# Twenty-four more zero products on TensorE around the first transposes and scores

## The chip, the cores and the metric

The kernel runs on one core of a Trainium2 chip. The metric is the device time of one execution in microseconds (us); lower is better. A core has five engines that run their own queues of instructions in order and wait for one another by semaphores: TensorE (PE in the profile, with its weight loads on a row of their own, PEld), VectorE (DVE), ScalarE (ACT), GpSimd (POOL) and SyncE (SP), which issues most of the transfers. TensorE's clock can be granted in full or in part; the profile shows the granted share.

## The reference

Two layers follow each other: cosine attention, then a feed-forward layer with a hard-swish. The shapes are 8 batches, 12 heads, 448 positions, 64 values per head; the feed-forward layer takes 3584 tokens of 768 values through 2048.

```python
q_n = q / (norm(q) + 1e-06)              # per position, over 64 values
k_n = k / (norm(k) + 1e-06)
attn = softmax(q_n @ k_n.T / tau)        # tau = 0.1
x = (attn @ v) -> [3584, 768]            # heads side by side
h = x @ w_in                             # [3584, 2048]
g = h * clip(h + 3, 0, 6) / 6
out = g @ w_out                          # [3584, 768]
```

## The kernel before

**Tiles.** The attention works on twins: twin `i` is two heads of a batch, six twins per batch, 48 in all. Two consecutive twins share one item of `q` and one of `k`; item `j` is one load of 128 x 896 values. For each item the kernel loads it (`LQ`), squares it (`SQ`, on ACT, DVE or POOL), sums the squares (`RE`, DVE, L310), makes 1 / norm of them (`NO`, four small ACT instructions, L326 to L329) and multiplies by it (`NM`, L341, into `nrm`). For the first items TensorE then transposes `nrm` (`TR`, seven products with the identity, L398, into the PSUM bank Y or Z), and DVE or ACT copies the result out to `tT` for q (`CQ`) and to `kz` for k (`CK`, L418 and L420).

For each twin the scores come in four groups: `SC.i.0` to `SC.i.3` (L502, and L499 for the last group) put the products of `kz` and `tT` into one of two pairs of PSUM banks named SC, the last number being the pair. `EX` (L521, ACT) takes the exponentials into `att`, `VA` (L537) multiplies them by the values `vx` into the accumulator PV, and `FI` (L557 and L558, DVE) divides by the sums. `VC` casts a twin's values into `vx` (L363 on POOL, L361 on DVE). `BK` and `CX` transpose the finished twin back into `xT`, from which the feed-forward layer's products (L671, L837, L1026) read. Weights are loaded by POOL (`W`, L1131).

**Order.** Nothing schedules the work: the list of strings `PLAN` is run word by word (L1198), and each word puts its instructions at the end of their engines' queues. A word such as `TR.1.Y` is an operation, a number and options; `a`, `v` or `p` names the engine (ACT, DVE, POOL). So an instruction's place in its engine's queue is its word's place in `PLAN`. Semaphores are set from the data that instructions share.

**The zero products.** The word `DP.n` calls `busy_pv(n)`. It issues `n` products of a block of zeros, 128 x 128 by 128 x 248, into columns of PV that nobody reads. The zeros lie in the first slice of `xT[1]`, which is not yet in use, and a memset at L1185 makes them.

```python
def busy_pv(n):
    first = ("VA", 0, 0) not in issued
    for _ in range(n):
        nc.tensor.matmul(
            PV[:, 0, 260:508], zeros[:, 0:128], zeros[:, 0:248], start=first, stop=first, skip_group_check=True
        )
```

Before the change there are 42 of them, all in the first 37 us: `DP.23` ahead of the first transpose `TR.0.Z`, `DP.10` ahead of `TR.1.Y`, `DP.3` after `SC.0.1`, `DP.2` ahead of `VA.0.0`, `DP.1` after `SC.1.3`, and `DP.3` ahead of `VA.5.0`.

Of the kernel before, what the change touches and what calls it, by code (L numbers as in the profile page):

```python
# [20 lines left out]
    "SQ.2.a.0.7 LQ.3 NM.0.v.0 NM.0.v.1 NO.0.1 DP.23 TR.0.Z RE.2 LQ.4 LQ.5 NM.1.p.0 NM.1.p.1 SQ.3.a.0.7 RE.3 SQ.5.p.0.7 DP.10 TR.1.Y CQ.0.a CK.0.v",  # L21
    "SQ.4.a.0.7 NO.1 CQ.1.a SC.0.0.0 NM.2.p EX.0.0 SC.0.1.1 EX.0.1 RE.4 DP.3 SC.0.2.0 W.0 LV.0 VC.0.p RE.5 CK.1.v SC.0.3.1 EX.0.2 NM.3.v LV.1 EX.0.3 NO.2",
    "VC.2.v W.2 TR.2.Z LQ.7 SC.1.0.0 EX.1.0 SC.1.1.1 EX.1.1 SQ.7.v.0.7 CQ.2.v VC.1.p DP.2 VA.0.0 VA.0.1 VA.0.2 SC.1.2.0 EX.1.2 VC.3.p NM.4.p VA.0.3 FI.0",
    "LQ.8 LQ.6 TR.3.Y CK.2.v SC.1.3.1 DP.1 SC.2.0.0 SQ.6.a.0.7 VA.1.0 VA.1.2 EX.1.3 SC.2.1.1 NM.5.p RE.7 EX.2.0 EX.2.1 CK.3.v VA.1.3 RE.6 SQ.8.p.0.7 VA.1.1",
    "SC.2.2.0 FI.1 EX.2.2 SC.2.3.1 EX.2.3 TR.4.Y VA.2.0 NO.3 LV.2 CQ.3.v SC.3.0.0 CQ.4.v CQ.5.v VC.4.v VA.2.1 VA.2.2 VA.2.3 SC.3.1.1 FI.2 TR.5.Z EX.3.0",
    "EX.3.1 CK.4.v BK.0.Y LV.3 LQ.9 RE.8 SC.3.2.0 SC.3.3.1 VA.3.0 EX.3.2 SC.4.0.0 EX.3.3 EX.4.0 CK.5.v CX.0.v SQ.9.v.0.7 VA.3.2 SC.4.1.1 VA.3.1 SC.4.2.0",
    "VA.3.3 FI.3 BK.2.Z CX.2.v EX.4.1 EX.4.2 NM.6.p TR.6.Y SC.4.3.1 EX.4.3 SC.5.0.0 EX.5.0 VA.4.0 RE.9 W.3 W.1 VA.4.3 SC.5.1.1 VC.6.p VA.4.2 VA.4.1 CQ.7.v",
    "CQ.6.v SC.5.2.0 EX.5.1 EX.5.2 NM.7.p TR.7.Z CK.6.v VC.5.p LQ.10 BK.3.Y CX.3.v SQ.10.p.0.7 SC.5.3.1 CS.7.v EX.5.3 NO.4 BK.1.Y FI.4 DP.3 VA.5.0 CS.6.v",
    "OPEN VA.5.2 SC.6.0 CX.1.v CK.7.v NM.8.p EX.6.0 VA.5.3 VA.5.1 FI.5 SC.6.1 EX.6.1 BK.4 CX.4.v SC.6.2 SC.6.3 EX.6.2 EX.6.3 BK.5 CX.5.v VA.6.0 VA.6.1 TR.8",
    "CQ.8.v CQ.9.v LQ.11 SQ.11.p.0.7 SC.7.0 VA.6.2 EX.7.0 VA.6.3 SC.7.1 SC.7.2 F.0.2 EX.7.1 EX.7.2 RE.11 RE.10 SC.7.3 EX.7.3 FA.0.2 F.0.7 FA.0.7 FI.6",  # L30
    "NM.9.p TR.9 CK.9.v CK.8.v CS.8.v CS.9.v F.0.1 LQ.14 LQ.13 SQ.13.a.0.7 NO.5 F.0.3 FA.0.1 FV.0.7 FV.0.2 FV.0.1 VC.7.p W.5 FA.0.3 LQ.12 LV.4 SQ.12.p.0.7",
    "SC.8.0 SC.8.1 FV.0.3 RE.12 LV.5 W.4 VC.8.p VA.7.0 EX.8.0 EX.8.1 NM.10.p F.0.0 FA.0.0 SC.8.2 VA.7.3 FV.0.0 VA.7.1 VA.7.2 VC.11.p EX.8.2 SC.8.3 EX.8.3",
    "SC.9.0 EX.9.0 F.0.4 RE.13 FI.7 SC.9.1 NM.11.p VC.10.p FA.0.4 FV.0.4 SC.9.2 TR.10 VA.8.0 VA.8.1 EX.9.1 NO.6 NM.13.p SC.9.3 CQ.11.v TR.11 CQ.10.v",
    "CS.11.v EX.9.2 EX.9.3 CK.11.v LQ.15 VA.8.2 F.0.6 VA.8.3 CS.10.v CK.10.v SC.10.0 FA.0.6 FV.0.6 EX.10.0 F.0.5 FA.0.5 SC.10.1 SC.10.2 SC.10.3 FI.8 VC.9.p",
    "VA.9.0 VA.9.2 VA.9.1 EX.10.1 EX.10.2 EX.10.3 FV.0.5 VA.9.3 FI.9 SC.11.0 EX.11.0 F.0.10 FA.0.10 FV.0.10 SQ.14.a.0.7 NM.12.p W.9 VA.10.0 TR.12 CQ.13.v",
    "CQ.12.v VA.10.1 SC.11.1 VA.10.3 SC.11.2 XP.6 VA.10.2 FI.10 EX.11.1 EX.11.2 F.0.14 FA.0.14 BK.8 SC.11.3 EX.11.3 CX.8.a BK.9 VA.11.0 TR.13 VA.11.2 RE.14",
    "CS.12.a CX.9.v LV.6 FV.0.14 CK.12.v CS.13.a CK.13.v F.0.15 FA.0.15 VC.12.p SQ.15.p.0.7 FV.0.15 SC.12.0 SC.12.1 RE.15 EX.12.0 EX.12.1 VA.11.1 F.0.13",
    "SC.12.2 VA.11.3 FI.11 FA.0.13 FV.0.13 BK.10 CX.10.a NO.7 F.0.12 FA.0.12 EX.12.2 F.0.9 W.8 LQ.16 SQ.16.v.6.1 SQ.16.p.0.6 RE.16 VA.12.0 BK.11 CX.11.v",
    "NM.15.p NM.14.p FV.0.12 F.0.8 LQ.20 LQ.17 LQ.19 SQ.17.a.0.7 RE.17 FA.0.8 SC.12.3 FV.0.8 G.6.0.p FA.0.9 FV.0.9 F.1.4 FA.1.4 EX.12.3 FV.1.4 F.1.1 FA.1.1",
    "FV.1.1 SC.13.0 SC.13.1 SQ.19.v.0.7 RE.19 EX.13.0 EX.13.1 LQ.18 SQ.18.p.0.7 F.1.5 FA.1.5 FV.1.5 LV.7 XD.15 XD.14 W.7 W.6 F.1.9 FA.1.9 FV.1.9 F.0.11",  # L40
    "VA.12.3 VC.13.a WS.7.1 FA.0.11 FV.0.11 F.1.15 FA.1.15 F.1.6 G.1.0.p G.2.0.p FA.1.6 RE.18 FV.1.15 CS.14.v FV.1.6 NO.8 NM.16.p F.1.8 SC.13.2 CK.15.v",
    "VA.12.1 LQ.21 SQ.21.p.0.7 VC.15.p SC.13.3 VA.12.2 FA.1.8 FV.1.8 FI.12 VC.14.a F.1.0 NM.17.v WS.y4.1 EX.13.2 EX.13.3 NO.9 F.1.10 CK.14.v FA.1.10",
    "FV.1.10 FA.1.0 NM.18.p GL.0.p FV.1.0 F.1.11 FA.1.11 SC.14.0 FV.1.11 EX.14.0 F.1.12 FA.1.12 FV.1.12 SC.14.1 SC.14.2 F.1.3 SQ.20.a.0.7 FA.1.3 G.7.0.v",
    "EX.14.1 EX.14.2 VA.13.0 VA.13.3 VA.13.2 VA.13.1 FI.13 FV.1.3 F.1.7 FA.1.7 FV.1.7 XD.16 SC.14.3 SC.15.0 VA.14.0 VA.14.2 VA.14.1 EX.14.3 EX.15.0 XD.17",
    "WS.6 SC.15.1 SC.15.2 VA.14.3 SC.15.3 EX.15.1 EX.15.2 F.1.2 FA.1.2 CK.16.v SC.16.0 EX.15.3 FI.14 CK.17.v FV.1.2 WS.y3 EX.16.0 LV.8 VC.16.a F.1.13",
    "FA.1.13 XP.12 LV.9 VA.15.0 VA.15.2 VA.15.3 SC.16.1 EX.16.1 SC.16.2 VA.15.1 NM.19.p CS.16.v XD.18 XD.19 FV.1.13 FI.15 F.1.14 FA.1.14 VC.17.a SC.16.3",
    "P.3.1 FV.1.14 LQ.22 XP.14 EX.16.2 WS.7.0 WS.y4.0 LQ.23 VA.16.0 SC.17.0 VA.16.1 G.5.0.p P.3.0 LV.11 RE.21 EX.16.3 VA.16.3 G.7.1.v EX.17.0 PE.3.1.a",
    "SC.17.1 SC.17.2 VA.16.2 CK.18.v PE.3.0.a EX.17.1 FI.16 XB.16 EX.17.2 P.5.0 PE.5.0.a SC.17.3 VA.17.0 RE.20 WS.1 VA.17.1 EX.17.3 SC.18.0 SC.18.1 EX.18.0",
    "EX.18.1 SC.18.2 VA.17.3 VA.17.2 G.5.1.p P.4.0 P.5.1.a FI.17 XB.17 NO.10 NM.20.v PE.4.0.v CK.19.v CS.18.v XD.20 LQ.24 LQ.25 VC.18.a P.1.0 P.7.0 EX.18.2",
    "BO.0 LV.10 SQ.22.a.0.7 G.1.1.p P.2.0 PE.2.0.a PE.1.0.v PE.7.0.v RS.0 SC.18.3 VA.18.0 NM.21.p XD.21 P.6.0 RE.22 PE.6.0.v SQ.23.a.0.7 RE.23 G.6.1.v",  # L50
    "LQ.26 VA.18.1 SC.19.0 EX.18.3 PE.5.1.a EX.19.0 VA.18.2 F.2.2 FA.2.2 FV.2.2 SQ.24.v.0.7 SC.19.1 SC.19.2 EX.19.1 EX.19.2 VA.18.3 FI.18 CK.21.v CK.20.v",
    "F.2.3 F.2.12 NO.11 FA.2.12 G.2.1.p FA.2.3 FV.2.3 NM.22.p LQ.27 PL.5.1 SC.19.3 FV.2.12 CS.20.v P.4.1 EX.19.3 XD.22 VC.19.v LV.12 F.2.13 FA.2.13 FV.2.13",
    "P.2.1.a F.2.14 VA.19.0 VA.19.2 F.2.5 NM.23.p LQ.28 XD.23 PE.2.1.a PE.4.1.v PL.2.1 VC.21.p BO.1 RS.1 SQ.25.a.0.7 F.2.11 VC.20.p RE.24 RE.25 VA.19.1",
    "FA.2.14 FV.2.14 FA.2.5 SQ.26.a.0.7 FA.2.11 F.2.6 FV.2.5 FV.2.11 VA.19.3 SC.20.0 SC.20.1 FA.2.6 FV.2.6 P.1.1 PE.1.1.v FI.19 EX.20.0 EX.20.1 SC.20.2",
    "VC.22.a NO.12 SC.20.3 F.2.9 CK.22.v FA.2.9 FV.2.9 EX.20.2 EX.20.3 P.6.1 PE.6.1.v F.2.7 XP.18 FA.2.7 FV.2.7 VA.20.0 VA.20.3 RE.26 SC.21.0 SC.21.1",
    "NM.24.v P.7.1 EX.21.0 LQ.29 LV.13 SC.21.2 SC.21.3 G.7.2.p NM.25.p VC.23.p EX.21.1 EX.21.2 VA.20.2 VA.20.1 G.6.2.p G.2.2.v PE.7.1.v SQ.27.a.0.7 RE.27",
    "F.2.8 CK.23.v CS.22.v XD.24 LQ.30 P.3.2 SC.22.0 VC.24.a EX.21.3 FA.2.8 FI.20 SQ.28.v.0.7 FV.2.8 RE.28 G.5.2.p PE.3.2.a EX.22.0 SQ.29.v.0.7 F.2.15",
    "FA.2.15 FV.2.15 NO.13 VA.21.0 P.5.2 PE.5.2.a VA.21.1 P.4.2 VA.21.3 PE.4.2.a BO.2 SC.22.1 SC.22.2 EX.22.1 EX.22.2 VA.21.2 RE.29 FI.21 XD.25 P.2.2",
    "PE.2.2.a SC.22.3 G.1.2.v NM.26.v VA.22.0 VA.22.1 SC.23.0 EX.22.3 SC.23.1 SC.23.2 VA.22.3 EX.23.0 EX.23.1 VA.22.2 CK.25.v FI.22 F.2.1 FA.2.1 SC.23.3",
    "FV.2.1 CK.24.v P.1.2 VA.23.0 F.2.4 XP.20 CS.24.v SQ.30.p.0.7 XD.26 PE.1.2.v NO.14 EX.23.2 EX.23.3 RS.2 NM.27.v LQ.32 LQ.31 P.6.2 VA.23.2 FA.2.4 FV.2.4",  # L60
    "SC.24.0 VA.23.3 PE.6.2.v SC.24.1 XD.27 SC.24.2 VA.23.1 EX.24.0 FI.23 P.3.3 NM.28.p NM.29.p EX.24.1 EX.24.2 SC.24.3 EX.24.3 PE.3.3.a XB.23 XB.22 P.7.2",
    "PE.7.2.v VC.25.p LQ.33 VA.24.0 VA.24.2 SC.25.0 SC.25.1 VC.26.a EX.25.0 SC.25.2 EX.25.1 VA.24.3 VA.24.1 EX.25.2 FI.24 G.1.3.v RE.30 F.2.10 SC.25.3",
    "EX.25.3 FA.2.10 CK.26.v FV.2.10 CK.27.v CS.26.v F.2.0 FA.2.0 FV.2.0 P.4.3 PE.4.3.a VA.25.0 VA.25.1 SC.26.0 SC.26.1 SC.26.2 VA.25.3 EX.26.0 VA.25.2",
    "G.7.3.v G.5.3.v G.6.3.v FI.25 EX.26.1 EX.26.2 SQ.32.a.0.7 SQ.31.p.0.7 F.3.11 F.3.12 FA.3.12 FA.3.11 P.5.3.a SC.26.3 EX.26.3 PE.5.3.a RE.31 G.7.4.v",
# [1170 lines left out]
```

## Time and profile before

| what | value |
|---|---|
| time, median of 3 runs | 400.42 us (399.2 to 400.69) |
| the profiled execution | 400.38 us |
| its span, from the first instruction to the last | 398.5 us |
| granted TensorE clock, mean over the span | 0.989 |
| busy share of the span | PE 96%, DVE 78%, POOL 75%, ACT 74% |
| shares of the chain that ended last | PE 85%, DVE 6%, ACT 3%, DMA 2% |

The span leaves 1.9 us of the profiled execution's time outside it. In the rows of the profile, the first number is the start and the second the time that the row covers; rows of equal instructions that follow each other are merged, with their count behind an x. In square brackets stands the time for which the engine was idle before the row, and what ended that. A product's row lasts from its issue until its last value has left the array, and the next product starts before that, so that the rate is read from start to start.

### The profile page before, as it was taken

To read this page: it belongs to the slowest core of one execution; us is meant where nothing else is said; L and a number is where in the kernel's file an instruction comes from. 1 tells how busy PE (TensorE), PEld (TensorE's weight loads), DVE (VectorE), ACT (ScalarE), POOL (GpSimd) and SP (SyncE) were. 2 spreads that over 40 slices of the span, in tenths; PEclk is the share of its full clock that TensorE was granted. 3 is DMA by queue.
4 is the path that set the end of the run, shared out by engine and by line. 5 is a ranking of instruction groups with operands and counts; after the bars stand their busy time and mean duration, and the time that the engine had idled before them with its cause. 6 is when DMAs were issued, how large, how long until landed. Compare 5 with 4: busy or idle time off the path is not lost.

```text
span 398.5 us, 9978 instructions
## 1 busy us (share of the span) xinstructions
PE 384.1 (96%) x3762; PEld 239.8 (60%) x3762; DVE 309.8 (78%) x545; ACT 295.6 (74%) x670; POOL 297.7 (75%) x269
## 2 busy tenths in 40 slices
PE   5798999999999999999999999999999999999995
PEld 4466556545655556655555555655566679977763
DVE  5898877998969698687766968854878968986862
ACT  5998999989966888896757876897787567744420
POOL 3999885899679947477839694778798988675752
PEclk9799999999999999999999999999999999999999
DMA  7999989997898779896896597666568350012124
GB/s 239 345 237 236 221 214 273 182 160 165 208 211 228 187 179 192 198 228 164 194 213 140 144 203 183 179 157 129 116 127 130 83 122 2 2 40 61 39 61 118
DMA packets 90271, 64.87 MB, mean 163 GB/s; under 512 B 55792, under 2 KB 89456, under 8 KB 90224
## 3 DMA queue, kind: packets, MB, share of 16 engines
q1 hardware_dynamic: 85312, 57.56, 59.4%
q0 software_dynamic: 4512, 6.29, 9.5%
q8 instruction: 29, 0.48, 0.5%
q10 hardware_dynamic: 400, 0.39, 0.3%
q14 instruction: 18, 0.15, 0.1%
HBM read 46.73 MB, written 11.01 MB: 145 GB/s over the span
## 4 chain that ended last, share of the span: by engine, by line
PE 85%; DVE 6%; ACT 3%; DMA 2%; issue 1%; POOL 1%; SPq 0%; DVEq 0%; POOLq 0%; ACTq 0%
PE M L671 18%; PE M L837 16%; PE PV L537 10%; PE V L837 6%; PE M L1026 6%; PE M L502 6%; PE Y L837 4%; PE Z L837 4%; PE Y L671 4%; PE Z L671 3%; PE Y L502 2%; PE Z L502 2%; DMA big<-in_q_dram 1%; DVE on L558 1%; PE Y L1026 1%
## 5 line engine op out<-in xcount | busy, mean ns | idle before, releaser
L521 ACT ACTIVATE att<-M 128x448 bf16<-128x448 f32 x193 | 95.8, 563 | 13.9 <-PE M L502 12.3
L671 PE MATMUL M<-xT,w_in_sb 128*128 128x448 bf16 x396 | 82.9, 353 | 0.0
L671 PEld LDWEIGHTS <-w_in_sb 128*128 128x128 bf16 x576 | 53.1, 98 | 46.8 <-issue 3.4
L341 POOL TENSOR_TENSOR nrm<-big,r 128x896 bf16<-128x896 f32 (+1 forms) x36 | 61.6, 1718 | 17.9 <-ACT r L329 14.5
L537 PEld LDWEIGHTS <-att 128*128 128x128 bf16 (+1 forms) x1536 | 56.4, 97 | 22.7 <-issue 9.9
L537 PE MATMUL PV<-vx,att 128*128 128x65 bf16 (+1 forms) x1536 | 64.9, 194 | 0.1
L837 PEld LDWEIGHTS <-gT 128*128 128x128 bf16 x448 | 42.9, 98 | 28.0 <-POOL gT L812 0.8
L310 DVE TENSOR_REDUCE n<-big 128x14 f32<-128x896 f32 (+1 forms) x50 | 51.6, 1042 | 3.2 <-ACT big L296 2.0
L686 DVE SCALAR_TENSOR_TENSOR gT<-u,M 128x448 bf16<-128x448 bf16 x66 | 39.5, 615 | 18.7 <-ACT u L680 18.4
L680 ACT ACTIVATE u<-M 128x448 bf16<-128x448 f32 x66 | 35.8, 556 | 10.8 <-PE M L671 9.7
L837 PE MATMUL M<-w_out_sb,gT 128*128 128x384 bf16 x224 | 40.4, 326 | 0.0
L298 POOL TENSOR_TENSOR big<-big 128x896 f32<-128x896 f32 (+2 forms) x19 | 31.4, 1655 | 11.7 <-DMA out_dram<-o 3.9
L837 PEld LDWEIGHTS <-gs 128*128 128x128 bf16 x296 | 28.1, 98 | 18.8 <-issue 1.3
L812 POOL TENSOR_TENSOR gT<-gT 128x1024 bf16<-128x1024 bf16 x15 | 31.9, 2123 | 9.5 <-DVE gs L812 9.0
L558 DVE TENSOR_TENSOR on<-PV,rc 128x512 bf16<-128x512 f32 x48 | 33.2, 691 | 1.6
L837 PE MATMUL M<-w_sum,gs 128*128 128x384 bf16 (+1 forms) x192 | 34.0, 323 | 0.0
L502 PE MATMUL M<-tT,kz 64*128 64x448 bf16 (+1 forms) x171 | 33.2, 354 | 0.6 <-DVE gT L686 0.4
L868 POOL TENSOR_TENSOR big<-big 128x384 f32<-128x384 f32 x14 | 18.3, 1304 | 17.8 <-ACT big L625 15.0
L812 POOL TENSOR_TENSOR gs<-gT 128x1024 bf16<-128x1024 bf16 x14 | 29.7, 2123 | 2.4 <-DVE gT L686 1.2
L521 ACT ACTIVATE att<-Z 128x448 bf16<-128x448 f32 x51 | 28.6, 561 | 1.3 <-PE M L502 1.0
L521 ACT ACTIVATE att<-Y 128x448 bf16<-128x448 f32 x50 | 28.1, 563 | 1.2 <-PE Z L502 1.2
L458 POOL COPY km<-tT 64x128 bf16<-64x128 bf16 x34 | 16.3, 481 | 12.6 <-PE Y L502 5.1
(146 smaller groups left out, 755.9 us busy)
## 6 DMA issues: line engine op xcount, KB each, us to landing
big<-in_q_dram SPq DMA_DIRECT2D x23, 448.0 KB, 4.7
big<-in_k_dram SPq DMA_DIRECT2D x23, 448.0 KB, 4.5
out_dram<-o SPq DMA_DIRECT2D x107, 96.0 KB, 2.2
big<-in_v_dram SPq DMA_DIRECT2D x68, 128.0 KB, 3.2
big<-in_v_dram SPq DMA_DIRECT2D x7, 448.0 KB, 7.2
w_out_sb<-in_moe_w_out_dram POOLq DMA_DIRECT2D x4, 768.0 KB, 10.4
w_in_sb<-in_moe_w_in_dram POOLq DMA_DIRECT2D x4, 384.0 KB, 5.8
w_in_sb<-in_moe_w_in_dram POOLq DMA_DIRECT2D x2, 768.0 KB, 7.9
```

The lines of the kernel that those rows point to most:

```text
L298: engines[e].tensor_tensor(out=o, in0=i, in1=i, op=ALU.mult)
L310: nc.vector.tensor_reduce(out=n2s[d % 2][:, j % 2, c], in_=sq[:, :, :, :].rearrange("p g c d -> p (g c) d")[:, c, :], axis=AX.X, op=ALU.add,)
L341: engines[e].tensor_tensor(out=nrm[:, :, g, :].rearrange("p c g d -> p g c d"), in0=raw_of[j][:, g, :, :], in1=rs[d % 2][3][:, j % 2, :] . ...
L502: nc.tensor.matmul(o, ks, qt[rows], start=True, stop=True)
L521: nc.scalar.activation(out=o, in_=x, func=AF.Exp, scale=inv_tau)
L537: nc.tensor.matmul(pv_out(j, h), at[rows, n, q_cols(i // HP, j)], vt[rows, 3 + h if name == "M" else 5 * h + int(name[1]), :], start=(name ...
L558: nc.vector.tensor_tensor(out=on[:, :, :, :].rearrange("p j h d -> p h j d"), in0=pv4[:, :, :, 0:D], in1=rc[:, :, :].to_broadcast([128, 2, ...
L671: nc.tensor.matmul(ps[:, 0:S], w_in_sb[:, cc, fc * 128 : (fc + 1) * 128], x[:, cc, 0:S], start=(cc == 0), stop=(cc == CC - 1),)
L680: nc.scalar.activation(out=u[:, :], in_=ps[:, 0:S], func=AF.Relu, bias=0.5, scale=1.0 / 6.0)
L686: nc.vector.scalar_tensor_tensor(out=g[:, fc, c0 : c0 + S], in0=u[:, :], scalar=1.0, in1=ps[:, 0:S], op0=ALU.min, op1=ALU.mult,)
L812: engines[e].tensor_tensor(out=o[:, :, :], in0=x, in1=y, op=op)
L837: nc.tensor.matmul(m, lhs[:, c, :], rhs[:, c, c0 : c0 + width], start=(base is None and c == 0), stop=(c == KC - 1), skip_group_check=True,)
```

## The change

Three words of `PLAN` change; the lines behind them are only broken at other places. The word ahead of `TR.1.Y` asks for 26 zero products and not 10, and two new words `DP.4` stand right after `TR.1.Y` and right after `SC.0.2.0`. No operation other than these is added, removed or moved.

```diff
-    "SQ.2.a.0.7 LQ.3 NM.0.v.0 NM.0.v.1 NO.0.1 DP.23 TR.0.Z RE.2 LQ.4 LQ.5 NM.1.p.0 NM.1.p.1 SQ.3.a.0.7 RE.3 SQ.5.p.0.7 DP.10 TR.1.Y CQ.0.a CK.0.v",
-    "SQ.4.a.0.7 NO.1 CQ.1.a SC.0.0.0 NM.2.p EX.0.0 SC.0.1.1 EX.0.1 RE.4 DP.3 SC.0.2.0 W.0 LV.0 VC.0.p RE.5 CK.1.v SC.0.3.1 EX.0.2 NM.3.v LV.1 EX.0.3 NO.2",
+    "SQ.2.a.0.7 LQ.3 NM.0.v.0 NM.0.v.1 NO.0.1 DP.23 TR.0.Z RE.2 LQ.4 LQ.5 NM.1.p.0 NM.1.p.1 SQ.3.a.0.7 RE.3 SQ.5.p.0.7 DP.26 TR.1.Y DP.4 CQ.0.a CK.0.v",
+    "SQ.4.a.0.7 NO.1 CQ.1.a SC.0.0.0 NM.2.p EX.0.0 SC.0.1.1 EX.0.1 RE.4 DP.3 SC.0.2.0 DP.4 W.0 LV.0 VC.0.p RE.5 CK.1.v SC.0.3.1 EX.0.2 NM.3.v LV.1 EX.0.3",
```

On TensorE's queue, at the second transpose `TR.1.Y`: the end of the zero products ahead of it (the weights `xT_70` are the zeros, `nrm_90` is the normalised item 1).

```order
+L1142 LDWEIGHTS xT_70
+L1142 MATMUL PV<-xT_70 128x248
 L398 LDWEIGHTS nrm_90
 L398 MATMUL Y<-ident,nrm_90 128x128
...
 L398 LDWEIGHTS nrm_90
 L398 MATMUL Y<-ident,nrm_90 128x128
+L1142 LDWEIGHTS xT_70
+L1142 MATMUL PV<-xT_70 128x248
```

Sixteen more pairs of this kind now stand ahead of the seven transposes, and four behind them, where the first scores of twin 0 (`SC.0.0`) followed at once.

On TensorE's queue, between the third and the fourth group of scores of twin 0 (`SC_135` and `SC_136` are the two pairs of banks, L499 is the last group).

```order
 L502 LDWEIGHTS kz_80
 L502 MATMUL SC_135<-tT_84,kz_80 128x448
+L1142 LDWEIGHTS xT_70
+L1142 MATMUL PV<-xT_70 128x248
...
 L499 LDWEIGHTS kz_80
 L499 MATMUL SC_136<-tT_84,kz_80 64x448
```

Four pairs now stand between the two groups, which followed each other before. The queues of DVE, ACT, POOL and SP keep their order.

188 rows, old and new, of the table PLAN are left out of this document.

## The prediction

> **What bounds the kernel now.** I read the page first: its span and its row of the granted clock, in 40 slices of 10 us.
>
> ```profile
> span 398.5 us, 9978 instructions
> PEclk9799999999999999999999999999999999999999
> ```
>
> The clock is short in one place, the second slice, and a little in the third. Then the table by stretches tells who is full when (time, then the busy time of each engine with its count, and the granted clock).
>
> ```profile
> 20.00:30.00 10.00, 9.37 (x146) 6.32 (x142) 9.34 (x20) 9.55 (x17) 9.81 (x10) 0.93 0.90 235
> 50.00:394.00 344.00, 343.63 (x3288) 213.94 (x3288) 268.71 (x458) 253.84 (x584) 256.83 (x216) 1.00 0.67 150
> ```
>
> From 50 us to the end PE is busy for 343.63 of 344 us at the full clock: what starts PE's dense part earlier or later moves the end by as much. From 20 to 30 us PE, DVE, ACT and POOL are all over 93% busy, POOL most. So the edit, which lies between 9 and 16 us, pays only what passes through that crowd. Next the same table cut at the edges of the slow stretch, which I found by narrowing the stretches, with PE's columns alone (busy time, count, clock, transfers).
>
> ```profile
> 7.79:11.21 3.42, 1.62 (x17) 1.00 0.99 348
> 11.21:14.62 3.41, 1.54 (x14) 1.00 1.05 390
> 14.62:18.03 3.41, 2.99 (x17) 0.50 1.07 375
> 18.03:21.45 3.42, 3.42 (x45) 0.50 1.16 178
> 21.45:24.86 3.41, 3.15 (x50) 1.00 0.98 222
> ```
>
> The clock is halved from 14.62 to 21.45, right behind 6.8 us in which PE was busy for 1.62 and 1.54 of 3.4 us (47 and 45%). It came back after a piece that was busy throughout. PE's timeline shows the pauses and what the half clock costs.
>
> ```profile
> 2.51 4.93 PE L1142 MATMUL PV<-xT 128*128 128x248 bf16 x23 [2.51 <-DVE xT L1185]
> 9.09 0.56 PE L398 MATMUL Z<-ident,nrm 128*128 128x128 bf16 x7 [1.64 <-DVE nrm L341]
> 9.49 1.22 PE L1142 MATMUL PV<-xT 128*128 128x248 bf16 x10
> 12.36 0.56 PE L398 MATMUL Y<-ident,nrm 128*128 128x128 bf16 x7 [1.65 <-POOL nrm L341]
> 13.41 0.55 PE L502 MATMUL SC<-tT,kz 64*128 64x448 bf16 x4 [0.49 <-ACT r L329]
> 14.79 0.56 PE L502 MATMUL SC<-tT,kz 64*128 64x448 bf16 x2 [0.40 <-ACT att L521]
> 15.60 0.58 PE L499 MATMUL SC<-tT,kz 64*64 64x448 bf16 x2 [0.25 <-ACT att L521]
> 16.11 0.93 PE L398 MATMUL Z<-ident,nrm 128*128 128x128 bf16 x7
> 17.83 0.60 PE L1142 MATMUL PV<-xT 128*128 128x248 bf16 x2
> 18.22 1.53 PE L537 MATMUL PV<-vx,att 128*128 128x65 bf16 x24
> 19.68 0.55 PE L502 MATMUL SC<-tT,kz 64*128 64x448 bf16 x2
> 20.03 0.42 PE L537 MATMUL PV<-vx,att 64*128 64x65 bf16 x8
> ...
> 24.92 0.40 PE L537 MATMUL PV<-vx,att 128*128 128x65 bf16 x8
> ...
> 25.55 0.89 PE L537 MATMUL PV<-vx,att 128*128 128x65 bf16 x24
> 26.28 0.35 PE L502 MATMUL SC<-tT,kz 64*128 64x448 bf16 x2
> ...
> 33.84 0.56 PE L398 MATMUL Z<-ident,nrm 128*128 128x128 bf16 x7
> ```
>
> The same work has two prices: seven transposes 0.93 or 0.56 us, 24 products with the values 1.53 or 0.89, a pair of scores 0.55 or 0.35. Who waits for PE there is seen on DVE and ACT.
>
> ```profile
> 19.17 0.39 DVE L420 COPY tT<-Z 128x448 bf16<-128x448 bf16 x1
> 20.50 0.21 DVE L557 RECIPROCAL rc<-PV 128x8 f32<-128x8 f32 x1 [0.94 <-PE PV L537]
> ...
> 29.83 1.47 DVE L298 TENSOR_TENSOR big<-big 128x896 f32<-128x896 f32 x1
> ...
> 34.44 0.36 DVE L420 COPY kz<-Z 128x384 bf16<-128x384 bf16 x1 [0.41 <-PE Z L398]
> ```
>
> ```profile
> 13.82 2.97 ACT L521 ACTIVATE att<-SC 128x896 bf16<-128x896 f32 x4
> ...
> 20.28 0.92 ACT L521 ACTIVATE att<-SC 128x896 bf16<-128x896 f32 x1 [0.93 <-PE SC L502]
> ```
>
> Both idle for 0.9 us, once, ended by PE in the slow stretch.
>
> **The added products by themselves.** Their length is in the answer on their line.
>
> ```profile
> L1142 PE MATMUL PV<-xT x42: 266/414/414, 2.5 to 36.9; 128*128 128x248 bf16 x42
> ```
>
> The shortest takes 0.27 us and the longest 0.41 from issue to end. Ten fast ones in 1.22 us are (1.22 - 0.27) / 9 = 0.106 us apart; 23 slow ones in 4.93 are (4.93 - 0.41) / 22 = 0.205 apart, so the clock came up between 7.44 and 9.09.
>
> Sixteen more ahead of `TR.1` take 16 x 0.106 = 1.70 us. The ten end their issue at 10.44 + 0.106 = 10.55, the sixteen at 12.24; `TR.1` starts at 12.36, held by POOL's `nrm`. They fit, with 0.12 us to spare: cost nothing. The four behind `TR.1` can start once the transposes have been fed, about 0.16 before their row ends, at 12.76, and take 0.42, to 13.18; the scores start at 13.41, held by the copy into `kz` and ACT. Nothing again. The four behind `SC.0.2` start at the latest when its row ends at the fast price, 14.79 + 0.35 = 15.14, and take 0.42, to 15.56; the next scores start at 15.60, held by ACT. Nothing, if the clock is full; at half clock (row end 15.35, four at 0.205) they would end at 16.17 and cost 0.6 us.
>
> **What they do to the clock.** In 7.79 to 11.21 they add about 0.5 us of busy time, in 11.21 to 14.62 about 1.15 before `TR.1` and 0.45 behind it: 2.1 and 3.1 of 3.4 us, 62 and 92%, where 47 and 45% went before the drop. I take it that the clock holds at 14.62. In the next piece the rows at the fast price (scores 0.35 and 0.38, transposes 0.56, two pairs of scores 0.55, and six zero products with 0.64 plus two drains) come to about 2.6 us, 76%, still far above 47%.
>
> The Trainium skill ("TensorE: Matmul & The Clock Gate", "HAM oscillation — how this bites in real kernels") wants no idle gap above about 3.4 us and has the clock drop behind an idle window of that length. The longest pause behind the first products is 1.65 us, and the clock dropped all the same, so this trace does not agree with a rule on single gaps; by it these pauses, and filling them, would not matter, which is the first rival's time.
>
> **What the full clock is worth.** The products with the values at 18.22 cannot start much earlier, for they need POOL's cast of `vx`.
>
> ```profile
> 10.47 1.83 POOL L341 TENSOR_TENSOR nrm<-big,r 128x448 bf16<-128x448 f32 x2 [4.15 <-ACT r L329]
> ...
> 16.69 1.29 POOL L363 CAST vx<-big 64x512 bf16<-64x512 f32 x2
> ...
> 29.71 2.06 POOL L363 CAST vx<-big 64x512 bf16<-64x512 f32 x2
> 31.85 1.69 POOL L341 TENSOR_TENSOR nrm<-big,r 128x896 bf16<-128x896 f32 x1
> 33.60 1.27 POOL L363 CAST vx<-big 64x512 bf16<-64x512 f32 x2
> ```
>
> The cast ends at 17.98; say 18.05 for PE. From there, slow, the rows 1.53 + 0.55 + 0.42 = 2.50 overlapped to 20.45 - 18.22 = 2.23. Fast, 0.89 + 0.35 + 0.40 = 1.64, less the same 0.27, is 1.37: PE is done at 19.42, before DVE ends its copy at 19.56. So DVE's 0.94 us goes, and ACT's 0.93 with it. In both timelines no further row up to 33 us is marked with idle time, so 0.9 us is what this stage hands on.
>
> Then POOL is late next. It runs its own list, full at 9.81 of 10 us, and its multiplication for item 7 ends at 31.85 + 1.69 = 33.54. `TR.7` on PE (33.84) needs it, and DVE's `kz` copy at 34.44 needs `TR.7`. PE takes 0.06 us to follow POOL (`TR.1` at 12.36: POOL ended at 10.47 + 1.83 = 12.30). If POOL stays where it is, 33.84 - 33.60 = 0.24 us is all that arrives. But POOL's list has a soft place: two casts took 2.06 us at 29.71 beside DVE's square at 29.83 (1.47 us), and 1.27 at 33.60 without one. With DVE 0.9 us earlier the square stands at 28.9 and ends about 30.0 to 30.4, mostly beside POOL's issue of weights. Of the 0.79 us between nothing and all may go; I take 0.5, as about a third of the overlap stays.
>
> The sum: 0.24 + 0.5 = 0.74 us earlier at `TR.7`, carried to the end by the dense PE. On the profiled execution's 400.38 us (398.5 of span and 1.9 around it) this gives 399.6. Its bounds are 0.24 (400.1) and 0.94 (399.4). That execution lies 0.04 under the median of the runs, so no correction is needed.
>
> **The rivals.** First: nothing moves. Either the clock drops at 14.62 in spite of 92%, or POOL's list swallows the 0.24 as well. For it speaks that POOL, the fullest engine of 20 to 30 us, is untouched; against it the two idle times on DVE and ACT. Time 400.4.
>
> Second, slower: the added products run at the half clock. The clock came up between 7.44 and 9.09 in this execution, which leaves only 0.4 us before the ten; from the point where it comes up later than 9.49, each product costs 0.205 and not 0.106. All 26 cold are 5.33 us; from about 9.85 (behind cold transposes) they reach 15.2, and `TR.1` is 2.8 us late. The row of the exponentials at 13.82 moves by that; ACT's pause of 0.93 absorbs some, and 1.9 us is left: 402.3. The Trainium skill (same page, "What's actually happening") says that the window on which the clock is set runs freely and does not start with the kernel; no row here shows another execution's phase.
>
> Third, slower: the clock drops one or two windows later, in the dense stretch from 21.45. There 3.15 us are busy at the full clock; at the prices above (1.53 / 0.89 = 1.7) they would take 2.2 us more, and with the 0.7 gained the time is 401.9. It decides from where 76% busy is too little; 47% was enough for one window, so I hold it for unlikely.
>
> Fourth, a larger gain: POOL gives all its 0.79 and the waits behind `TR.7` close as well, or the drop costs more than its idle times show. The fastest run of before, 399.2, is 1.2 below the median; with 1.8 the time is 398.6.
>
> **How the numbers follow.** Forecast 0.66, nothing moves 0.14, cold products 0.08, later drop 0.07, larger gain 0.05. The likeliest case alone lies in 399.0 to 400.3, since the runs themselves scatter by some tenths. To hold 8 in 10 the range takes in the first rival and reaches into those on both sides: 398.5 to 401.9. Half a per cent, which is what a measurement here can tell, is 2.0 us, so faster begins under 398.4 and slower over 402.4. Under 398.4: 0.04 from the forecast and 0.03 from the larger gain, 0.07. Over 402.4: 0.04 each from the two slower rivals, 0.08. Within: 0.85.
>
> **What would show it.** Right: the clock row without its 7; zero products at about 0.106 from 9.49 to 12.24 with `TR.1` still at 12.3 to 12.4; 24 products with the values in 0.89 at about 18.1; no 0.9 us pause on DVE and ACT at 20; POOL's casts at 29.7 in under 2 us; `TR.7` at about 33.1. Wrong: a clock of 0.5 anywhere after 14 us, `TR.1` later than 12.5, or an early gain that is no longer there in PE's dense part at 50 us.

## The result and the profile after

| | kernel before | with the change |
|---|---|---|
| median of 20 runs | 400.19 us (399.2 to 402.64) | 401.1 us (399.24 to 403.15) |
| ratio to before, 95% interval | | 1.0027 (1.0015 to 1.004) |
| profiled execution, span | 400.38 us, 398.5 us | 401.06 us, 399.3 us |

The change makes the kernel slower by about 1.1 us. The time lies inside the stated range of 398.5 to 401.9, but the change is clear of the noise and goes the other way: 399.6 was forecast.

In the profile of the changed kernel the page's clock row has lost its 7, as forecast.

```profile
PEclk9999999999999999999999999999999999999999
```

The timeline of PE (start, time covered, count) shows where the time went instead.

```profile
2.51 4.93 PE L1142 MATMUL PV<-xT 128*128 128x248 bf16 x23 [2.51 <-DVE xT L1185]
9.09 0.93 PE L398 MATMUL Z<-ident,nrm 128*128 128x128 bf16 x7 [1.64 <-DVE nrm L341]
9.81 3.97 PE L1142 MATMUL PV<-xT 128*128 128x248 bf16 x26
13.62 0.55 PE L398 MATMUL Y<-ident,nrm 128*128 128x128 bf16 x7
14.01 0.59 PE L1142 MATMUL PV<-xT 128*128 128x248 bf16 x4
14.65 0.55 PE L502 MATMUL SC<-tT,kz 64*128 64x448 bf16 x4
...
18.60 0.90 PE L537 MATMUL PV<-vx,att 128*128 128x65 bf16 x24
```

The first transposes took 0.93 us, the half clock's price, and the 26 products 3.97 us and not 2.9. With 0.205 us for a slow step and 0.106 for a fast one, (3.97 - 0.27) us over 25 steps make 10 or 11 slow ones, so that the clock came up at about 12.0, and not before 9.09 as in the profile of before. `TR.1` starts at 13.62. On POOL's timeline the `nrm` that it needs (item 1) was ready at 10.14 + 1.84 = 11.98, so PE held it up for 1.64 us.

```profile
10.14 1.84 POOL L341 TENSOR_TENSOR nrm<-big,r 128x448 bf16<-128x448 f32 x2 [3.92 <-ACT r L329]
...
16.23 2.13 POOL L363 CAST vx<-big 64x512 bf16<-64x512 f32 x2
18.30 0.66 POOL L1131 DMA_DIRECT2D w_in_sb<-in_moe_w_in_dram  x1
...
30.38 1.93 POOL L363 CAST vx<-big 64x512 bf16<-64x512 f32 x2
32.39 1.69 POOL L341 TENSOR_TENSOR nrm<-big,r 128x896 bf16<-128x896 f32 x1
```

ACT's timeline shows the wait passed on: the first exponentials start at 15.06, 1.24 us later than before, behind an idle time of 1.58 that PE ended.

```profile
15.06 2.97 ACT L521 ACTIVATE att<-SC 128x896 bf16<-128x896 f32 x4 [1.58 <-PE SC L502]
...
18.88 2.51 ACT L521 ACTIVATE att<-SC 128x896 bf16<-128x896 f32 x3
```

The pause of 0.93 us that ACT had at 20.28 is gone, as forecast (the row at 18.88 runs through it); it takes up most of the delay. What stays comes by POOL. Its casts at 16.23 now meet a later multiplication on DVE (L341) and take 2.13 us, against 1.29 before, so its multiplication for item 7 ends at 32.39 + 1.69 = 34.08 and `TR.7` starts at 34.14, 0.30 us later than before. PE's dense part keeps these 0.30. The other 0.5 us of the span are one wait, at 216.

```profile
216.03 1.15 PE L837 MATMUL M<-w_out_sb,gT 128*128 128x384 bf16 x6 [0.50 <-POOL gT L812]
```

This wait is not the change's: a second profile of the kernel before has it too, with 0.41 us, and one of a run below (eighteen products ahead of `TR.1`) with 0.88, and it is missing in nine of the thirteen profiles of this case, the whole change with more products ahead of `TR.0` among them. Its row in the second profile of before:

```profile
215.11 1.47 PE L837 MATMUL M<-w_out_sb,gT 128*128 128x384 bf16 x8 [0.41 <-POOL gT L812]
```

In this execution, then, the span is 0.8 us longer, 0.3 of it by way of `TR.7`, than in a profile of before in which the clock had dropped. That one pair of profiles does not tell which of the 24 products cost, nor whether the late clock is the rule. The theories for the runs were: A, the sixteen products ahead of `TR.1` hold it up where the clock comes up late; B, the clock drops later, in dense work, and this costs.

### The profile page after: what moved, and what is told of

The parts are those of the page before. It is cut to its first block, busy times and chain, and to the rows that moved or that the text cites. A ratio compares the mean times of both kernels' runs of the same rounds, so it can differ in the third digit from the quotient of the medians.

```text
span 399.3 us, 10026 instructions
## 1 busy us (share of the span) xinstructions
PE 385.7 (97%) x3786; PEld 241.6 (61%) x3786; DVE 309.7 (78%) x545; ACT 295.5 (74%) x670; POOL 299.0 (75%) x269
## 4 chain that ended last, share of the span: by engine, by line
PE 82%; POOL 4%; DVE 4%; ACT 4%; DMA 3%; issue 2%; SPq 0%; POOLq 0%; DVEq 0%; ACTq 0%
PE M L837 16%; PE M L671 16%; PE PV L537 10%; PE V L837 6%; PE M L1026 6%; PE M L502 5%; PE Y L671 4%; PE Z L837 4%; PE Y L837 4%; PE Z L671 3%; ACT att L521 3%; DMA big<-in_k_dram 2%; PE Y L502 2%; PE Z L502 1%; POOL nrm L341 1%
## 5 line engine op out<-in xcount | busy, mean ns | idle before, releaser
L341 POOL TENSOR_TENSOR nrm<-big,r 128x896 bf16<-128x896 f32 (+1 forms) x36 | 61.7, 1720 | 15.7 <-ACT r L329 14.2
L537 PEld LDWEIGHTS <-att 128*128 128x128 bf16 (+1 forms) x1536 | 55.5, 97 | 22.5 <-issue 9.7
L537 PE MATMUL PV<-vx,att 128*128 128x65 bf16 (+1 forms) x1536 | 64.1, 193 | 0.0
L837 PEld LDWEIGHTS <-gT 128*128 128x128 bf16 x448 | 42.9, 98 | 28.5 <-POOL gT L812 1.3
L298 POOL TENSOR_TENSOR big<-big 128x896 f32<-128x896 f32 (+2 forms) x19 | 31.5, 1657 | 13.8 <-DMA big<-in_k_dram 8.3
L837 PE MATMUL M<-w_out_sb,gT 128*128 128x384 bf16 x224 | 40.5, 326 | 0.5 <-POOL gT L812 0.5
L837 PEld LDWEIGHTS <-gs 128*128 128x128 bf16 x296 | 28.1, 98 | 18.8 <-issue 1.3
L837 PE MATMUL M<-w_sum,gs 128*128 128x384 bf16 (+1 forms) x192 | 34.0, 323 | 0.0
```

Of the source, the lines that this page charges most:

```text
L298: engines[e].tensor_tensor(out=o, in0=i, in1=i, op=ALU.mult)
L341: engines[e].tensor_tensor(out=nrm[:, :, g, :].rearrange("p c g d -> p g c d"), in0=raw_of[j][:, g, :, :], in1=rs[d % 2][3][:, j % 2, :] . ...
L537: nc.tensor.matmul(pv_out(j, h), at[rows, n, q_cols(i // HP, j)], vt[rows, 3 + h if name == "M" else 5 * h + int(name[1]), :], start=(name ...
L837: nc.tensor.matmul(m, lhs[:, c, :], rhs[:, c, c0 : c0 + width], start=(base is None and c == 0), stop=(c == KC - 1), skip_group_check=True,)
```

## The experiments

**The sixteen ahead of `TR.1` alone.**

```diff
-    DP.10 TR.1.Y
+    DP.26 TR.1.Y
```

> Only the sixteen products ahead of the second transpose are added. Theory A (in some executions the clock comes up only after 9.5 us, the products then run 0.205 us apart and hold the second transpose up by about 1.3 us, of which 0.3 to 0.8 us arrives at the end): slower than before by 0.15 to 0.3%, the whole loss of the change; in a profile with a late clock the second transpose starts at 13 us or later. Theory B (the loss comes from a later drop of the clock in the dense stretch, whatever stands ahead of the second transpose): no more than half of the loss here, and a half clock somewhere behind 16 us in the profile.

Ratio 1.0029 (1.0015 to 1.0044): the whole loss. The profile, from PE's timeline and the table by stretches (PE's busy time, count and clock), shows the products slow for another reason than in the changed kernel's.

```profile
2.51 4.06 PE L1142 MATMUL PV<-xT 128*128 128x248 bf16 x23 [2.51 <-DVE xT L1185]
9.18 0.93 PE L398 MATMUL Z<-ident,nrm 128*128 128x128 bf16 x7 [2.61 <-DVE nrm L341]
9.90 4.12 PE L1142 MATMUL PV<-xT 128*128 128x248 bf16 x26
13.85 0.55 PE L398 MATMUL Y<-ident,nrm 128*128 128x128 bf16 x7
```

```profile
5.52:8.93 3.41, 1.05 (x10) 1.00 1.02 365
8.93:12.34 3.41, 3.17 (x19) 0.50 1.04 389
12.34:390.00 377.66, 372.11 (x3712) 1.00 0.70 159
```

Here the clock came up early, at 5.52. The lead-in (the 23 products ahead of the first transposes) then ran out sooner, the pause ahead of the first transposes grew to 2.61 us, and behind a stretch that was busy for 1.05 of 3.41 us the clock was halved from 8.93 to 12.34, over the first half of the 26 products. Item 1 was ready at 12.0 and `TR.1` started at 13.85. From 12.34 to 390 the clock is full, so theory B falls for this execution. Each run comes with its mean clock. One half window (a stretch of 3.4 us at half clock) makes about 0.996 of 1: eleven of these twelve runs lie at 0.994 to 0.996, and so do twelve of the changed kernel's twenty. That their half window lies at the same place is inferred, for the runs without a profile show only the mean. The mean also leaves out the slow start ahead of the first grant on record, so that a late clock does not lower it, and takes in a half clock in the last microseconds, 0.003 at most in these profiles.

**The eight behind it alone.**

```diff
-    DP.10 TR.1.Y
+    DP.10 TR.1.Y DP.4
-    DP.3 SC.0.2.0
+    DP.3 SC.0.2.0 DP.4
```

> Only the two groups of four products behind the second transpose and behind the third group of scores are added. Theory A: they stand in pauses of 0.49 and 0.25 us and cost nothing, ratio 0.998 to 1.001. Theory B: the clock drops later than before, in dense work, ratio over 1.002.

Ratio 0.999 (0.9975 to 1.0005): no cost is seen, as A has it. In the profiled execution the clock came up at 7.62 and held through the dense part, and the span was 396.8 us. Eight of the twelve runs have a mean clock of 0.990 to 0.996, so the clock did not hold in all of them; whether a small cost and a small gain offset each other here is not shown.

**A longer lead-in, without the change.**

```diff
-    DP.23 TR.0.Z
+    DP.31 TR.0.Z
```

> The products of the change are left out; the lead-in has 31 zero products and not 23, so that it is busy from 2.5 to 9.1 us at half clock and a whole window of 3.4 us lies in it wherever the windows start. Theory A: the clock is always up when the first transpose is done, the ten products take 1.2 us in every execution; the drop behind 14 us stays, ratio 0.998 to 1.001. Theory B tells nothing else here.

Ratio 0.9972 (0.9958 to 0.9986): faster than both kernels, and more than was expected, because the drop behind 14 us did not stay: in the profile there is none, and eleven of twelve runs have a mean clock of 0.996 or more, where 18 of the 35 runs of before beside them have 0.991 or less. PE's timeline at the second transposes, and POOL's at 29 us:

```profile
9.62 0.56 PE L398 MATMUL Z<-ident,nrm 128*128 128x128 bf16 x7 [2.05 <-DVE nrm L341]
10.02 1.22 PE L1142 MATMUL PV<-xT 128*128 128x248 bf16 x10
11.70 0.56 PE L398 MATMUL Y<-ident,nrm 128*128 128x128 bf16 x7 [0.46 <-POOL nrm L341]
...
17.24 0.89 PE L537 MATMUL PV<-vx,att 128*128 128x65 bf16 x24 [0.38 <-POOL vx L363]
```

```profile
28.91 1.52 POOL L363 CAST vx<-big 64x512 bf16<-64x512 f32 x2
30.51 1.69 POOL L341 TENSOR_TENSOR nrm<-big,r 128x896 bf16<-128x896 f32 x1
```

The pause ahead of `TR.1` is 0.46 us here, not 1.65: the first transposes came later and item 1 earlier.

**The whole change with that lead-in.**

> The whole change with a lead-in of 31 products. Theory A: the products are never at half clock, the second transpose starts at about 12.3 us, the clock holds, and the gain that was forecast shows: ratio 0.997 to 0.999, mean clock 0.998 in nearly all runs. Theory B: the drop in the dense stretch stays, mean clock 0.994 to 0.996 in most runs as with the change, ratio over 1.001.

Ratio 0.9999 (0.9983 to 1.0014). Theory A missed: the mean clock is 0.997 or more in eleven of twelve runs, in the profile the products ran fast, and the gain did not come.

```profile
9.74 0.56 PE L398 MATMUL Z<-ident,nrm 128*128 128x128 bf16 x7 [1.61 <-DVE nrm L341]
10.14 2.92 PE L1142 MATMUL PV<-xT 128*128 128x248 bf16 x26
12.89 0.55 PE L398 MATMUL Y<-ident,nrm 128*128 128x128 bf16 x7
```

At the full clock the 26 products take 26 x 0.106 = 2.76 us, from 10.14 to 12.89, and item 1 was ready at 12.43. So they can be too long even without a late clock. This gave the second form of the theory, A2: the room between the first transposes and item 1 is another in each execution, mostly smaller than 2.76 us. Rival C was that something else about the sixteen costs, their number say, or that the eight cost too once the clock is up.

**Lead-in and the eight, without the sixteen.** The kernel of the last run with `DP.10` ahead of `TR.1`.

> Lead-in of 31, ten products ahead of the second transpose as before, the two groups of four behind: the change without its sixteen, with the lead-in. Theory A2 (26 products take 2.75 us even at full clock, while normalised item 1 comes 1.6 to 2.8 us after the first transposes, so that the sixteen push the second transpose back in most executions, and a late start there arrives at the end nearly whole): ratio 0.996 to 0.998, as the lead-in alone or better, and 0.2 to 0.4% below the whole change with the lead-in. Rival C (the loss of the sixteen is something else than their time in the queue, or the two groups behind cost as well): above 0.999.

Ratio 0.9981 (0.9968 to 0.9995), just above the expected range and not below the lead-in alone. Against 0.9999 the sixteen cost about 0.2%, 0.7 us, with the longer lead-in; the two intervals overlap a little, and the two kernels were measured in different series, each beside its own runs of before.

**Item 1 earlier.** As the last, with `DP.6`, and ACT's four small instructions moved:

```diff
-    SQ.2.a.0.7 LQ.3 NM.0.v.0 NM.0.v.1 NO.0.1 DP.31
+    LQ.3 NM.0.v.0 NM.0.v.1 NO.0.1 SQ.2.a.0.7 DP.31
```

> As the one before, with six products ahead of the second transpose, and the four small ACT instructions for item 1's norm ahead of the square of item 2, which waits for a transfer. Theory A2: normalised item 1 is ready about 1 us earlier, the second transpose starts at 10.7 to 11.2 us, and 0.5 to 1.0 us of it is still there at the end: ratio 0.994 to 0.997. Rival C: the start of the second transpose does not set the end; ratio as the one before.

Ratio 0.9991 (0.9978 to 1.0005), a miss. `TR.1` did start at 11.04, but the third transposes only at 15.48, against 15.25 in the run before. POOL's timeline tells why: its square had to wait for a sum on DVE that now came later.

```profile
9.15 1.83 POOL L341 TENSOR_TENSOR nrm<-big,r 128x448 bf16<-128x448 f32 x2 [2.70 <-ACT r L329]
12.10 1.68 POOL L298 TENSOR_TENSOR big<-big 128x896 f32<-128x896 f32 x1 [1.12 <-DVE n L310]
```

So `TR.1` no longer set the pace here; the next item did. But that item was late by this edit, which puts item 2's square behind item 1's norm. What an earlier `TR.1` alone would be worth is not shown.

**The same count, half as wide.** The whole change, with `busy_pv` writing 124 columns in `DP.26` alone:

```diff
+        first_n = n
...
-                PV[:, 0, 260:508], zeros[:, 0:128], zeros[:, 0:248], ...
+                PV[:, 0, 260 : 508 if first_n != 26 else 384], zeros[:, 0:128], zeros[:, 0 : 248 if first_n != 26 else 124], ...
```

The added line makes L1142 of the other kernels L1143 here.

> The whole change with the lead-in of 23, but the 26 products ahead of the second transpose are 124 columns wide and not 248: the same count of instructions and of weight loads, half the time on the array (about 2.8 us at half clock, 1.5 at full clock). Theory A2: the second transpose is late only at half clock, by 0.3 us or less; ratio 0.997 to 1.001. Rival C (the count of instructions or the queue matters, not their time): ratio 1.002 to 1.004 as with the change.

Ratio 1.0 (0.9982 to 1.0018): the loss is gone with the width, so it is the products' time on the array and not their number (the interval still touches the changed kernel's, 1.0015 to 1.004). In the profile they ran at half clock and `TR.1` was 0.7 us late, for item 1 was ready at 11.47: more than the 0.3 expected.

```profile
9.49 2.89 PE L1143 MATMUL PV<-xT 128*128 128x124 bf16 x26
12.18 0.79 PE L398 MATMUL Y<-ident,nrm 128*128 128x128 bf16 x7
```

**The changed kernel once more**, one execution.

> The changed kernel once more, for another execution's clock. Theory A2: wherever the clock comes up or drops, the second transpose starts when the 26 products have left the array, 12.7 us or later, and not when item 1 is ready (11.6 to 12.4).

402.67 us, span 400.9. The products were slow throughout.

```profile
9.39 0.93 PE L398 MATMUL Z<-ident,nrm 128*128 128x128 bf16 x7 [1.95 <-DVE nrm L341]
10.11 5.47 PE L1142 MATMUL PV<-xT 128*128 128x248 bf16 x26
15.42 0.55 PE L398 MATMUL Y<-ident,nrm 128*128 128x128 bf16 x7
```

They end at 15.4, with item 1 ready at 13.08: `TR.1` is 2.3 us late. The mean clock of this execution is 1.000, for the slow start does not count in it.

**The zeros first.** The products of the change are left out, the memset of the zeros stands ahead of the others on DVE, and the lead-in has 40.

```diff
+    zeros = xT[1][:, 0, :]
+    nc.vector.memset(zeros, 0.0)
     for t in vr:
...
-    zeros = xT[1][:, 0, :]
-    nc.vector.memset(zeros, 0.0)
...
-    DP.23 TR.0.Z
+    DP.40 TR.0.Z
```

> The products of the change are left out; the memset of the zeros comes first on DVE, so that the lead-in can start at about 1.1 us and not 2.5, and it has 40 products. Theory A2: the clock is up before 7.6 us wherever its windows start, the second transpose starts as soon as normalised item 1 is ready, ratio 0.996 to 0.998 as with a lead-in of 31. It is slower than that one only if the clock, up earlier, drops again in the longer pause ahead of the first transposes: then mean clocks of 0.994 to 0.996 in several runs and a ratio near 0.999.

Ratio 0.9983 (0.9969 to 0.9996), no better than the lead-in of 31. Three of twelve runs have a mean clock of 0.99 and two 0.996, so a drop does come back in some, as the second half of the expectation had it, though with two half windows and not one. The profile has no drop, so where it lies is open.

**Eight more instead of sixteen.** The whole change with the lead-in of 31 and `DP.18` ahead of `TR.1`.

> As the change with the lead-in of 31, but eight more and not sixteen more ahead of the second transpose: 18 products are 1.9 us at full clock and fit where item 1 comes 1.6 to 2.8 us after the first transposes. Theory A2: between the kernel with ten (0.9981) and the one with 26 (0.9999), nearer the former: 0.998 to 0.9995. Rival C (any more products ahead of it cost the same, or their number does not matter): 0.9999 or above, or 0.997.

Ratio 0.9974 (0.9962 to 0.9985), below the 0.998 that A2 gave as its least and nearer to the 0.997 of rival C's second form, that the number of products does not matter. Taken alone, this run does not decide between them; beside the 26 of the whole change with this lead-in (0.9999) and the sixteen alone (1.0029), more products do cost. In the profile the eighteen fit: they end as item 1 comes, at 11.72.

```profile
9.35 0.56 PE L398 MATMUL Z<-ident,nrm 128*128 128x128 bf16 x7 [0.96 <-DVE nrm L341]
9.75 2.07 PE L1142 MATMUL PV<-xT 128*128 128x248 bf16 x18
11.77 0.56 PE L398 MATMUL Y<-ident,nrm 128*128 128x128 bf16 x7
```

This kernel and the lead-in alone are the two fastest; their intervals do not part them.

**The kernel before once more**, one execution.

> The kernel before once more, for another execution. Theory A2: the second transpose follows normalised item 1 by about 0.06 us, at 11.6 to 12.4 us, so that the pause ahead of it, 1.65 us in the first profile, is another length; the clock is halved for one or two windows of 3.4 us somewhere before 25 us.

400.22 us, span 398.3. The clock was halved from 14.53 to 21.35, and the room ahead of `TR.1` was much smaller than in the first profile.

```profile
9.67 0.56 PE L398 MATMUL Z<-ident,nrm 128*128 128x128 bf16 x7 [2.23 <-DVE nrm L341]
10.07 1.22 PE L1142 MATMUL PV<-xT 128*128 128x248 bf16 x10
11.91 0.57 PE L398 MATMUL Y<-ident,nrm 128*128 128x128 bf16 x7 [0.62 <-POOL nrm L341]
```

What moves item 1 is seen on ACT. Its square of item 2 stands ahead of item 1's norm and needs a transfer of `q`, which it had to wait for in the first profile of before, and not in the second:

```profile
8.61 0.95 ACT L296 ACTIVATE big<-big 128x896 f32<-128x896 f32 x1 [1.05 <-DMA big<-in_q_dram]
```

```profile
8.15 0.95 ACT L296 ACTIVATE big<-big 128x896 f32<-128x896 f32 x1
```

In the second profile of the changed kernel it waited until 9.38, and item 1 came at 13.08.

All profiles, from their timelines (us; the last column is the wait of PE at L837, 214 to 217 us, where there is one):

| profile | first transposes | item 1 ready | room for products | products take | second transposes | span | late wait |
|---|---|---|---|---|---|---|---|
| before | 9.09 | 12.30 | 2.82 | 10: 1.06 | 12.36 | 398.5 | |
| before, again | 9.67 | 11.85 | 1.78 | 10: 1.06 | 11.91 | 398.3 | 0.41 |
| lead-in 31, the eight, item 1 earlier | 9.21 | 10.98 | 1.37 | 6: 0.64 | 11.04 | 397.0 | |
| lead-in 31 | 9.62 | 11.65 | 1.62 | 10: 1.06 | 11.70 | 396.7 | |
| lead-in 31, the eight | 9.29 | 11.63 | 1.94 | 10: 1.06 | 11.69 | 396.7 | |
| the eight alone | 9.22 | 11.71 | 2.09 | 10: 1.06 | 11.77 | 396.8 | |
| zeros first, lead-in 40 | 9.31 | 11.74 | 2.03 | 10: 1.06 | 11.80 | 396.8 | |
| lead-in 31, eighteen, the eight | 9.35 | 11.72 | 1.97 | 18: 2.0 | 11.77 | 398.0 | 0.88 |
| the change, half as wide | 8.99 | 11.47 | 2.08 | 26: 2.7 | 12.18 | 397.8 | |
| lead-in 31, the change | 9.74 | 12.43 | 2.29 | 26: 2.75 | 12.89 | 398.1 | |
| the change | 9.09 | 11.98 | 2.49 | 26: 3.8 | 13.62 | 399.3 | 0.50 |
| the sixteen alone | 9.18 | 12.02 | 2.44 | 26: 4.0 | 13.85 | 399.0 | |
| the change, again | 9.39 | 13.08 | 3.29 | 26: 5.3 | 15.42 | 400.9 | 0.47 |

The room is counted from 0.40 us behind the first transposes' start, the fast price, to item 1. In the two profiles of before the clock is halved behind 14 us; in the others it is not. From the lead-in of 31 to the last row `TR.1` moves by 3.72 us and the span, less the late wait, by 3.7: what `TR.1` loses arrives at the end nearly whole. The rows between lie within 0.4 us of that line, the half-wide products 0.6 above it.

## Why the prediction was wrong

- **The step that failed** is the first of the sum: "They fit, with 0.12 us to spare: cost nothing." It took the pause of 1.65 us ahead of `TR.1` from one execution as if it belonged to the kernel, and likewise the clock that was up at 9.49. Neither belongs to it. In the profiles of other executions the room was 1.4 to 2.5 us and only once more than the 2.76 that 26 fast products need, and that once they were slow. In both profiles of the changed kernel the clock came up too late for them. So `TR.1` started at 13.62 and 15.42 and not at 12.36. Measured, the sixteen cost 0.29% alone (1.0029) and about 0.2% even with the longer lead-in. The pause depends on when transfers land, as ACT's rows above show, which the argument left out. It asked whether the products fit, and not how far the neighbour times move from one execution to the next.
- **The slow products** were the second rival, given 0.08. Its mechanism, its place and its point of decision were right: the clock came up later than 9.49 in both profiles of the changed kernel, at about 12.0 and after 15, and the delay of `TR.1` was 1.6 and 2.3 us. Its price of 402.3 was too high for the first of them, 401.06, where only ten or eleven products were slow; the second, with all 26 slow as the rival had it, took 402.67, some of it by an item 1 that came later (13.08). What it missed is the other way into the same state, seen with the sixteen alone: a clock that comes up early ends the lead-in early and drops again in the pause. A chance of 0.08 for a state that may be the usual one (twelve of twenty means fit one half window) came from one profile too.
- **The eight behind `TR.1` and the scores** show no cost, as forecast (0.999).
- **What the clock would do behind 14 us** came out as forecast in the profiles: it does not drop there in any of the four with the whole change or the sixteen. But in them `TR.1` is later than forecast, so the stretches are not those of the working, and three of the changed kernel's runs have a mean clock of 0.989 to 0.991, two half windows; where these lie is open.
- **What the full clock is worth** was sized well. The lead-in alone against the second profile of before, both with `TR.1` near 11.8: POOL's casts at 29 us took 1.52 us and not 2.06 (0.54; 0.5 was taken), item 7 was ready 0.75 earlier and `TR.7` started at 32.26 and not 33.34. Of these 1.08 us, 0.21 are `TR.1`'s; the rest, 0.87, stands against 0.74 in the sum, inside its bounds of 0.24 to 0.94. This rests on one pair of profiles; the ratio of 0.9972, 1.1 us, is of that size. The change spent the gain ahead of `TR.1`. The second profile of before has these rows on POOL:

```profile
29.12 2.06 POOL L363 CAST vx<-big 64x512 bf16<-64x512 f32 x2
31.26 1.69 POOL L341 TENSOR_TENSOR nrm<-big,r 128x896 bf16<-128x896 f32 x1
```

- **The third rival**, a later drop in dense work, appears in no profile.
- The Trainium skill's free-running window ("TensorE: Matmul & The Clock Gate", "What's actually happening") agrees with the runs: with the same lead-in the clock came up at 7.6 to 7.8 us, 12.0 and 15.3, and at 5.5 and 5.8. That should have weighed more than a sentence.

What stays open is why the longer lead-in also removes the drop behind 14 us, and how often each state comes in the changed kernel. For the earlier drop one pair of profiles tells: the clock came up at 5.84 with the half-wide products (lead-in 23) and at 5.85 with the lead-in of 31. The next stretch of 3.41 us was busy for 1.15 us in the first and 1.73 in the second, and only the first was followed by a half clock.

## What to carry to other kernels

A pause in one profile is not room: before filling it, look in a second execution at how far the event on each side of it moves, and fill only the smallest. Filler that keeps a clock up is best put where the work behind it in the same queue waits longest in every execution: here 31 and not 23 products ahead of the first transposes gained (ratio 0.9972), 26 between the first and the second lost, and eighteen there did no harm that these runs show (0.9974). Price such filler at the slow clock, since it is there that it is needed.

## What the runs showed of the hardware

- At the start, the clock came up behind stretches of 3.41 us in which PE was busy for 84% or more (2.87 us in the changed kernel's profile, 3.01 with the sixteen alone), and not behind ones with 68 and 77%. The rows are of the changed kernel's profile; the clock column shows 1.00 there, for no grant was on record yet, and the products' rate shows the half clock:

```profile
1.72:5.13 3.41, 2.62 (x13) 1.00 0.87 244
5.13:8.55 3.42, 2.31 (x12) 1.00 1.01 354
8.55:11.96 3.41, 2.87 (x18) 1.00 1.05 393
```

- Behind a drop, the same share did not bring it up: in both profiles of before a stretch at half clock with 2.99 and 3.01 us busy (88%) was followed by another, and the clock came back behind that one, busy throughout.
- It dropped behind single stretches with 31 and 34% busy (the sixteen alone, the narrow products), and behind two with 47 and 45%, or 42 and 56%, in the two profiles of before; with the lead-in of 31 it held at 51 and 64%, and with the eight alone at 47 and 65%. One limit on the busy share of a stretch does not explain all of these.
- Two casts on POOL took 1.27 to 2.13 us. The long ones overlap a multiplication on DVE (L298 or L341): 2.06 at 29.71 before, 2.13 at 16.23 with the change. Beside DVE's own casts (L361) they took 1.29, at 16.69 before.
